# Loading q, k and v in float32 from another queue, casting on GpSimd, and two first layers ahead of the second

## The chip, the cores and the metric

The kernel runs on one core of one Trainium2 chip. What counts is the time of one execution in microseconds (us) on the device; several runs give a median. The profile of one execution gives a span, from its first to its last instruction. Engines: PE is TensorE (matmuls; PEld its weight loads), DVE is VectorE, ACT is ScalarE, POOL is GpSimd, SP is SyncE. PE, DVE, ACT, POOL and SP each run their own instructions in the order of their own queue and wait for one another by semaphores. Tiles lie in SBUF; PE writes into PSUM, which has eight banks per partition.

## What is computed

Causal attention with 8 heads of 64 over 768 positions, in 4 batches, followed by a feed-forward block whose activation is a squared ReLU. A query sees the 96 last positions (itself included) and the first 8 positions of the sequence; each head subtracts a slope times the distance from its scores (for the first positions, outside the window, the distance counts as 96).

```python
def _attn_ref(q, k, v, n_global, n_local):          # 4 x 8 x 768 x 64, 8, 96
    scores = scale * np.matmul(q, k.transpose(0, 1, 3, 2))
    rel = pos[:, None] - pos[None, :]
    is_global = pos[None, :] < int(n_global)
    is_local = (rel >= 0) & (rel < int(n_local))
    keep = is_global | is_local
    dist = np.where(is_global & ~is_local, float(n_local), np.abs(rel).astype(np.float32))
    scores = np.where(keep, scores - slopes[:, None, None] * dist[None], -1e9)
    a = softmax(scores)
    return np.matmul(a, v)

x = attn_out.transpose(0, 2, 1, 3).reshape(3072, 512)
h = np.maximum(x @ w_in, 0.0)                       # 512 x 2048
out = h * h @ w_out                                 # 2048 x 512
```

All inputs and the output are float32 in memory; inside, the matmuls take float16 and add up in float32.

## The kernel before

The work is cut into eight half batches (`hb` 0 to 7; `b, half = divmod(hb, 2)`), each with 384 query rows in three tiles of 128, and into four pairs of heads (`a` 0 to 3).

For each half batch `load` brings q, k and v: nine DMAs of one row tile each, issued on GpSimd's queue, which turn float32 into float16 on the way. q and k land in `sq` and `sk` (two buffers each), v lands in the batch's `v` tile, which has a column of ones beside each head. For the very first half batch each DMA takes four heads, so there are eighteen.

The attention of a half batch is a list of jobs. `fix_v` makes `vb`, a second form of the v tiles whose first 32 rows are those of the first positions. `prep(a)` transposes q and k of a pair on PE (`trp`), copies them out with ACT (`qk`) and builds `kb`, the corresponding second form of k, on DVE. `score` (two per pair) multiplies k with q into `sp`, ACT takes the exponential (`ex`), DVE multiplies by the mask (`phat`). `attend` multiplies `phat` with v into `av`, DVE divides by the sum (`rec`, `tm`). `to_x` transposes `tm` on PE and ACT copies it into `xt`. The list is skewed, so that `prep` of a pair stands before `score` of the one before it, and so on.

The feed-forward block of a half batch is another list: sixteen jobs `first` (layer 1: four matmuls each into `hps`; after each second one ACT makes `hr` by ReLU and DVE squares it into `h2`) and twelve jobs `second` (layer 2: four matmuls each into `yps`; DVE copies `y`, SP's queue stores it). `merge` spreads the attention of the next half batch over the feed-forward jobs of the present one. The PSUM pool for `sp`, `hps` and `yps` (`ps_big`) has three tiles, that for `trp`, `av` and `trx` two.

The masks (`fill_masks`) are made once, at the start: eight exponentials on ACT, and on DVE a few products over all eight heads. The weights, `w_in` and `w_out`, come in four parts each on GpSimd's queue, cast on the way.

Only PE's order is that of the program text (`manual_schedule(engines={PE})`); the other engines' instructions, DMA issues included, are put in order by the framework's scheduler from its own estimates.

Of the kernel before, what the change touches and what calls it, by code (L numbers as in the profile page):

```python
# [14 lines left out]
P = 128  # L15
# [17 lines left out]
def kernel(  # L33
# [22 lines left out]
    NHB = 2 * B  # L56
    GR = 32
# [16 lines left out]

    dist = const.tile([P, 2 * P], FP32, name="dist")
    distc = const.tile([P, 2 * P], FP32, name="distc")
# [3 lines left out]
    ge0 = const.tile([P, 2 * P], FP16, name="ge0")  # L80
    isg = const.tile([P, 1], FP32, name="isg")
    far = const.tile([P, 2 * P], FP16, name="far")
    decay = const.tile([P, H, 2 * P], FP16, name="decay")
    gw = const.tile([P, H, 2 * P], FP16, name="gw")
    cg = const.tile([P, H], FP16, name="cg")
# [3 lines left out]
    w_out_sb = const.tile([P, NFT, d_model], FP16, name="w_out_sb")  # L89

    def fill_index():
        nc.gpsimd.iota(dist, pattern=[[1, 2 * P]], base=0, channel_multiplier=-1,
                       allow_small_or_imprecise_dtypes=True)
        nc.gpsimd.iota(pidx, pattern=[[0, 1]], base=0, channel_multiplier=1,
                       allow_small_or_imprecise_dtypes=True)
        nc.vector.tensor_scalar(out=ident, in0=dist[:, 0:P], scalar1=0.0, scalar2=None,
                                op0=ALU.is_equal)

    def fill_masks():
        nc.vector.tensor_scalar(out=distc, in0=dist, scalar1=0.0, scalar2=None, op0=ALU.max)  # L100
        for h in range(H):
            nc.scalar.activation(out=decay[:, h, :], in_=distc, func=AF.Exp, scale=-slopes[h])
            nc.vector.memset(cg[:, h:h + 1], math.exp(-slopes[h] * NL))
        nc.vector.tensor_scalar(out=ge0, in0=dist, scalar1=0.0, scalar2=None, op0=ALU.is_ge)
        nc.vector.scalar_tensor_tensor(out=local, in0=dist, scalar=float(NL), in1=ge0,
                                       op0=ALU.is_lt, op1=ALU.mult)
        nc.vector.tensor_scalar(out=isg, in0=pidx, scalar1=float(NG), scalar2=None,
                                op0=ALU.is_lt)
        nc.vector.tensor_scalar(out=far, in0=local, scalar1=0.5, scalar2=isg,
                                op0=ALU.is_lt, op1=ALU.mult)  # L110
        nc.vector.tensor_tensor(out=gw, in0=far[:, None, :].to_broadcast([P, H, 2 * P]),
                                in1=cg[:, :, None].to_broadcast([P, H, 2 * P]), op=ALU.mult)
        own, bef = slice(0, P), slice(P, 2 * P)
        nc.vector.tensor_tensor(out=mask[:, :, P:3 * P], in0=decay,
                                in1=local[:, None, :].to_broadcast([P, H, 2 * P]), op=ALU.mult)
        nc.vector.tensor_tensor(out=mask[:, :, 0:P], in0=mask[:, :, P:2 * P],
                                in1=gw[:, :, own], op=ALU.add)
        nc.vector.tensor_tensor(out=mask[:, :, 2 * P:3 * P], in0=mask[:, :, 2 * P:3 * P],
                                in1=gw[:, :, bef], op=ALU.add)
        nc.vector.tensor_copy(out=mask[:, :, 3 * P:5 * P], in_=mask[:, :, P:3 * P])  # L120


# [4 lines left out]
    for b in range(B):  # L127
        bt = Batch()
        bt.sq = [None, None]
        bt.sk = [None, None]  # L130
        batches.append(bt)

    def load(b, half, h0, h1):
        bt = batches[b]
        if half == 0 and h0 == 0:
            bt.qk = qk_p.tile([P, 2, NPAIR, S], FP16, name="qk", tag="qk")
            bt.kb = qk_p.tile([P, NPAIR, NT - 1, P], FP16, name="kb", tag="kb")
            bt.v = qk_p.tile([P, NT, H, D + 1], FP16, name="v", tag="v")
            bt.vb = qk_p.tile([P, NT - 1, H, D + 1], FP16, name="vb", tag="vb")
            nc.vector.memset(bt.v[:, :, :, D:D + 1], 1.0)  # L140
        if h0 == 0:
            bt.sq[half] = stage_p.tile([P, HT, H, D], FP16, name="sq", tag="sq")
            bt.sk[half] = stage_p.tile([P, HT, H, D], FP16, name="sk", tag="sk")
# [17 lines left out]
    def prep(b, half, a):  # L161
        bt = batches[b]
        trp = ps_att.tile([P, 2, HT, P], FP16, name="trp", tag="att")
        for i, st in enumerate((bt.sq[half], bt.sk[half])):
            for t in range(HT):
                nc.tensor.transpose(out=trp[:, i, t, :], in_=st[:, t, 2 * a:2 * a + 2, :],  # L166
                                    identity=ident)
        nc.scalar.copy(out=bt.qk[:, :, a, half * HALF:(half + 1) * HALF],  # L168
                       in_=trp.rearrange("p i t c -> p i (t c)"))
        kt = bt.qk[:, 1, a, :].rearrange("p (t c) -> p t c", c=P)  # L170
        t0, t1 = (0, HT) if half == 0 else (HT, NT - 1)
        nc.vector.tensor_copy(out=bt.kb[:, a, t0:t1, GR:P], in_=kt[:, t0:t1, GR:P])  # L172
        nc.vector.tensor_copy(out=bt.kb[:, a, t0:t1, 0:GR],  # L173
                              in_=kt[:, 0:1, 0:GR].to_broadcast([P, t1 - t0, GR]))
# [67 lines left out]
    def attention(hb):  # L242
        b, half = divmod(hb, 2)
        A = list(range(NPAIR))
# [12 lines left out]


    def ffn(hb):
        t0 = hb * HALF  # L260
        st = {}
        jobs = []

        def first(i, m2):
            if i == 0 and m2 == 0:
                st["h2"] = h_p.tile([P, NFT, HALF], FP16, name="h2", tag="h2")
# [7 lines left out]
            if m2 == 1:  # L274
                hr = h_p.tile([P, 2, HALF], FP16, name="hr", tag="hr")
                nc.scalar.activation(out=hr, in_=st["ps"][:, :, 0:HALF], func=AF.Relu)  # L276
                nc.vector.tensor_tensor(out=st["h2"][:, 2 * i:2 * i + 2, :], in0=hr, in1=hr,
                                        op=ALU.mult)

        def second(j, m0):  # L280
            if j != 1 and m0 == 0:
                st["y"] = ps_big.tile([P, 2, 512], FP32, name="yps", tag="big")
            for m in range(m0, m0 + 4):
                nc.tensor.matmul(st["y"][:, j % 2, :], lhsT=st["h2"][:, m, j * P:(j + 1) * P],  # L284
                                 rhs=w_out_sb[:, m, :], start=m == 0, stop=m == NFT - 1)
            if m0 + 4 == NFT and j != 0:
                n = 2 if j == 1 else 1
                y = y_p.tile([P, 2, d_model], FP32, name="y", tag="y")
                nc.vector.tensor_copy(out=y[:, 0:n, :], in_=st["y"][:, 0:n, :])  # L289
# [4 lines left out]
        for i in range(NFT // 2):  # L294
            for m2 in range(2):
                jobs.append(lambda i=i, m2=m2: first(i, m2))
        for j in range(HT):
            for m0 in range(0, NFT, 4):
                jobs.append(lambda j=j, m0=m0: second(j, m0))
        return jobs  # L300
# [13 lines left out]
    fill_index()  # L314
    for h0 in range(0, H, 4):
        load(0, 0, h0, h0 + 4)
    fill_masks()
    for c in range(4):
        load_w_in(c)
    load(0, 1, 0, H)  # L320
    for c in range(4):
        load_w_out(c)
    load(1, 0, 0, H)
    with tc.manual_schedule(engines={PE}):
        for job in attention(0):
            job()
        for hb in range(NHB):
            if 1 <= hb and hb + 2 < NHB:
                load((hb + 2) // 2, hb % 2, 0, H)
            main = ffn(hb)  # L330
            side = attention(hb + 1) if hb + 1 < NHB else []
            for job in merge(main, side, 1, len(main) - 4):
                job()
# [35 lines left out]
```

## Time and profile before

| | |
|---|---|
| three runs | 260.56, 260.62 (median), 261.44 us |
| span of the profiled execution | 258.2 us |
| granted TensorE clock, mean | 0.986 of full speed |
| DMA on GpSimd's queue (q0) | 79,248 packets, 13.64 MB written |
| DMA on SP's queue (q1) | 3,328 packets, 6.29 MB written |
| read from HBM | 27.26 MB |

The profile gives no time of the execution other than its span; the median of the runs lies 2.4 us above it. A line of the groups reads: line of the program, engine, operation, output and inputs, shape and count; then busy time in us and the mean of one in ns; then the idle time ahead of them and what ended it. A window's line gives, after its length, each engine's busy time, the granted clock, the DMA share and GB/s as written. The slices cut the span into 40 parts of 6.5 us, with the busy share in tenths.

### The profile page before, as it was taken

Reading aid. Unit: us, or ns where it says so; the run is one execution under the profiler, and the core shown is the slowest. Engines: PE = TensorE matmul, PEld = TensorE weight load, DVE = VectorE, ACT = ScalarE, POOL = GpSimd, SP = SyncE. Lnnn points to the kernel's source line nnn. Section 1 sums busy time; section 2 is a strip of 40 time slices with the busy share of each in tenths; the row PEclk is TensorE's granted clock in tenths of the full one; section 3 lists DMA queues with packets and bytes.
Section 4 is the critical chain, followed back from the end, with each engine's and each line's share of the span. In section 5 each row is a group of like instructions: output and inputs, shape, how many; then the busy total and the mean of one; then the engine's idle time right before and its main releaser. Section 6 shows DMA issues by size and latency. Waiting matters only on the chain.

```text
span 258.2 us, 4590 instructions
## 1 busy us (share of the span) xinstructions
PE 227.6 (88%) x1888; PEld 125.0 (48%) x1888; DVE 139.6 (54%) x331; ACT 135.0 (52%) x201; POOL 75.9 (29%) x95
## 2 busy tenths in 40 slices
PE   1428769928999999999699999999999999999994
PEld 0216345514555555645455555655654565555541
DVE  8558237454778336746676436843675346543411
ACT  5436359601297329941587329831984179623600
POOL 8996573696207000528008000700000000000000
PEclk9999999985999999999999999999999999999999
DMA  6999999999909930499909630792100210003003
GB/s 44 87 116 205 169 179 208 156 153 109 209 1 63 62 121 3 29 96 76 169 3 84 41 122 3 50 76 81 43 0 0 85 41 3 0 5 119 0 3 122
DMA packets 82597, 20.22 MB, mean 78 GB/s; under 512 B 75408, under 2 KB 79504, under 8 KB 82576
## 3 DMA queue, kind: packets, MB, share of 16 engines
q0 software_dynamic: 79248, 13.64, 71.0%
q1 hardware_dynamic: 3328, 6.29, 6.6%
q8 instruction: 15, 0.25, 0.4%
q14 instruction: 6, 0.05, 0.1%
HBM read 27.26 MB, written 6.29 MB: 130 GB/s over the span
## 4 chain that ended last, share of the span: by engine, by line
PE 54%; DMA 17%; ACT 11%; POOL 11%; DVE 3%; issue 2%; DVEq 0%; POOLq 0%
PE yps L284 27%; PE hps L272 19%; DMA v<-in_v_dram 8%; POOL v L149 5%; DMA w_out_sb<-in_moe_w_out_dram 5%; DMA w_in_sb<-in_moe_w_in_dram 5%; ACT hr L276 4%; ACT ex L205 4%; PE av L220 3%; ACT qk L168 3%; PE sp L201 3%; POOL sq L149 2%; POOL sk L149 2%; PE trx L239 1%; POOL w_out_sb L310 1%
## 5 line engine op out<-in xcount | busy, mean ns | idle before, releaser
L272 PE MATMUL hps<-xt,w_in_sb 128*128 128x384 f16 x512 | 98.5, 329 | 2.6 <-DVE y L289 1.9
L276 ACT ACTIVATE hr<-hps 128x768 f16<-128x768 f32 x64 | 52.8, 825 | 43.9 <-PE hps L272 43.0
L272 PEld LDWEIGHTS <-w_in_sb 128*128 128x128 f16 x512 | 45.9, 98 | 31.4 <-issue 3.2
L205 ACT ACTIVATE ex<-sp 128x768 f16<-128x768 f32 x64 | 47.8, 779 | 8.9 <-PE sp L201 8.8
L149 POOL DMA_DIRECT2D sq<-in_q_dram x27 | 23.4, 882 | 71.0 <-PE trp L166 70.5
L206 DVE TENSOR_TENSOR phat<-ex,mask 128x768 f16<-128x768 f16 x64 | 33.0, 523 | 20.5 <-ACT ex L205 17.1
L240 ACT COPY xt<-trx 128x384 f16<-128x384 f16 x32 | 15.3, 478 | 41.1 <-PE trx L239 41.1
L168 ACT COPY qk<-trp 128x768 f16<-128x768 f16 x32 | 25.2, 808 | 15.3 <-PE trp L166 15.3
L289 DVE COPY y<-yps 128x1024 f32<-128x1024 f32 (+1 forms) x16 | 15.3, 958 | 26.3 <-PE yps L284 26.2
L149 POOL DMA_DIRECT2D v<-in_v_dram x27 | 23.3, 883 | 16.3 <-DVE rec L225 8.2
L149 POOL DMA_DIRECT2D sk<-in_k_dram x27 | 23.1, 878 | 4.1 <-DMA w_out_sb<-in_moe_w_out_dram 2.0
L220 PEld LDWEIGHTS <-phat 128*128 128x128 f16 x352 | 15.9, 102 | 16.4 <-DVE tm L227 6.2
L220 PE MATMUL av<-v,phat 128*128 128x65 f16 x192 | 16.4, 201 | 6.8 <-DVE tm L227 5.7
L166 PE MATMUL trp<-ident,sq 128*128 128x128 f16 x96 | 12.4, 229 | 7.4 <-DMA sq<-in_q_dram 7.4
L220 PE MATMUL av<-vb,phat 128*128 128x65 f16 x160 | 15.7, 200 | 3.3 <-DVE vb L157 3.3
L227 DVE TENSOR_TENSOR tm<-av,rec 128x384 f16<-128x384 f32 x32 | 17.8, 556 | 0.9
L201 PE MATMUL sp<-qk 64*128 64x128 f16 x192 | 17.7, 231 | 0.3 <-ACT qk L168 0.3
L201 PE MATMUL sp<-qk,kb 64*128 64x128 f16 x160 | 16.4, 227 | 1.7 <-DVE kb L173 1.7
L166 PE MATMUL trp<-ident,sk 128*128 128x128 f16 x96 | 12.4, 229 | 4.3 <-DMA sk<-in_k_dram 4.2
L172 DVE COPY kb<-qk 128x288 f16<-128x288 f16 (+1 forms) x32 | 10.2, 320 | 9.3 <-ACT qk L168 6.9
L201 PEld LDWEIGHTS <-qk 64*128 64x128 f16 x192 | 8.0, 97 | 14.8 <-issue 12.6
L166 PEld LDWEIGHTS <-sq 128*128 128x128 f16 x96 | 8.3, 101 | 12.3 <-DMA sq<-in_q_dram 8.8
(56 smaller groups left out, 246.6 us busy)
## 6 DMA issues: line engine op xcount, KB each, us to landing
out_dram<-y SPq DMA_DIRECT2D x8, 512.0 KB, 2.8
sq<-in_q_dram POOLq DMA_DIRECT2D x21, 128.0 KB, 5.7
sk<-in_k_dram POOLq DMA_DIRECT2D x21, 128.0 KB, 5.3
v<-in_v_dram POOLq DMA_DIRECT2D x21, 128.0 KB, 6.4
w_in_sb<-in_moe_w_in_dram POOLq DMA_DIRECT2D x4, 512.0 KB, 8.6
w_out_sb<-in_moe_w_out_dram POOLq DMA_DIRECT2D x4, 512.0 KB, 10.5
out_dram<-y SPq DMA_DIRECT2D x8, 256.0 KB, 2.0
sq<-in_q_dram POOLq DMA_DIRECT2D x6, 64.0 KB, 3.0
```

The lines of the kernel that those rows point to most:

```text
L149: nc.gpsimd.dma_start(out=dst[:, t, h0:h1, :], in_=src[b, h0:h1, r0:r0 + P, :].rearrange("h p d -> p h d"))
L166: nc.tensor.transpose(out=trp[:, i, t, :], in_=st[:, t, 2 * a:2 * a + 2, :], identity=ident)
L168: nc.scalar.copy(out=bt.qk[:, :, a, half * HALF:(half + 1) * HALF], in_=trp.rearrange("p i t c -> p i (t c)"))
L201: nc.tensor.matmul(sp[:, e, i * P:(i + 1) * P], lhsT=lhsT, rhs=bt.qk[rows, 0, a, r * P:(r + 1) * P], start=True, stop=True)
L205: nc.scalar.activation(out=ex[:, :, 0:n], in_=sp[:, :, 0:n], func=AF.Exp, scale=scale)
L206: nc.vector.tensor_tensor(out=phat[:, :, c0:c0 + n], in0=ex[:, :, 0:n], in1=mask[:, 2 * a:2 * a + 2, m0:m0 + n], op=ALU.mult)
L220: nc.tensor.matmul(av[:, e, j, :], lhsT=phat[:, e, i * P:(i + 1) * P], rhs=bt.vb[:, r - 1, h, :] if before else bt.v[:, r, h, :], start=n ...
L227: nc.vector.tensor_tensor(out=tm.rearrange("p t e d -> p e t d"), in0=av[:, :, :, 0:D], in1=rec[:, :, :, None].to_broadcast([P, 2, HT, D]) ...
L240: nc.scalar.copy(out=xts[hb][:, a, :], in_=trp.rearrange("p t c -> p (t c)"))
L272: nc.tensor.matmul(st["ps"][:, m2, 0:HALF], lhsT=w_in_sb[:, kk, m * P:(m + 1) * P], rhs=xt[:, kk, :], start=kk == 0, stop=kk == NCT - 1)
L276: nc.scalar.activation(out=hr, in_=st["ps"][:, :, 0:HALF], func=AF.Relu)
L284: nc.tensor.matmul(st["y"][:, j % 2, :], lhsT=st["h2"][:, m, j * P:(j + 1) * P], rhs=w_out_sb[:, m, :], start=m == 0, stop=m == NFT - 1)
```

## The change

q, k and v are now loaded without a cast: float32 goes into new `raw` tiles (six buffers for q and k, which take four heads each; six for v), on SP's queue, and for one half batch on ACT's. A piece of q or k is three successive rows of the sequence in one partition, 768 bytes in one run; v keeps its row tiles. GpSimd then casts into `sq`, `sk` (three buffers) and `v`; for the first half batch DVE casts q, two heads at a time. Since a transposed tile now holds every third row, ACT's copy into `qk` writes with a stride of three. The masks are made one pair at a time, between the casts and jobs of the first attention. `fix_v` moves behind `prep(1)`'s place in the list. Layer 1 of half batches 0 and 1 comes first, then layer 2 of half batch 0, with its parts of the inner sum in the outer loop, and of 1. `w_in` and `w_out` stay on GpSimd's queue with their cast: two parts of `w_in` ahead of the casts of the second half batch, the rest behind them. The order of every engine is the program's.

```diff
-    stage_p = ctx.enter_context(tc.tile_pool(name="stage", bufs=2))
+    raw_p = ctx.enter_context(tc.tile_pool(name="raw", bufs=6))
+    stage_p = ctx.enter_context(tc.tile_pool(name="stage", bufs=3))
...
+    def fill_mask(a):
+        hs = slice(2 * a, 2 * a + 2)
+        for h in (2 * a, 2 * a + 1):
+            nc.scalar.activation(out=decay[:, h, :], in_=distc, func=AF.Exp, scale=-slopes[h])
+        nc.vector.tensor_tensor(out=mask[:, hs, P:3 * P], in0=decay[:, hs, :],
+                                in1=local[:, None, :].to_broadcast([P, 2, 2 * P]), op=ALU.mult)
+        for h in (2 * a, 2 * a + 1):
+            nc.vector.scalar_tensor_tensor(
+                out=mask[:, h, 0:4 * P].rearrange("p (x c) -> p x c", c=2 * P)[:, :, 0:P],
+                in0=far.rearrange("p (x c) -> p x c", c=P), scalar=math.exp(-slopes[h] * NL),
+                in1=mask[:, h, P:3 * P].rearrange("p (x c) -> p x c", c=P),
+                op0=ALU.mult, op1=ALU.add)
+        nc.vector.tensor_copy(out=mask[:, hs, 3 * P:5 * P], in_=mask[:, hs, P:3 * P])
...
-        for src, dst in ((q, bt.sq[half]), (k, bt.sk[half]),
-                         (v, bt.v[:, half * HT:(half + 1) * HT, :, 0:D])):
-            for t in range(HT):
-                r0 = half * HALF + t * P
-                nc.gpsimd.dma_start(
-                    out=dst[:, t, h0:h1, :],
-                    in_=src[b, h0:h1, r0:r0 + P, :].rearrange("h p d -> p h d"))
+        for name, src in (("q", q), ("k", k)):
+            if o == 0:
+                bt.raw[half, name, g] = raw_p.tile([P, HH, HT, D], FP32, name="r" + name,
+                                                   tag="rqk")
+            (eng or nc.sync).dma_start(
+                out=bt.raw[half, name, g][:, o:o + n].rearrange("p h t d -> p h (t d)"),
+                in_=src[b, h0:h0 + n, rows, :].rearrange("h (p t) d -> p h (t d)", t=HT))
...
+    def load(b, half):
+        load_qk(b, half, 0, HH)
+        for t in range(HT):
+            load_v(b, half, t)
+        load_qk(b, half, HH, HH)
...
+    def cast(b, half):
+        if half == 0:
+            open_batch(b)
+        cast_qk(b, half, 0, HH, (nc.gpsimd, nc.gpsimd))
+        for t in range(HT):
+            cast_v(b, half, t)
+        cast_qk(b, half, HH, HH, (nc.gpsimd, nc.gpsimd))
...
-        nc.scalar.copy(out=bt.qk[:, :, a, half * HALF:(half + 1) * HALF],
-                       in_=trp.rearrange("p i t c -> p i (t c)"))
+        nc.scalar.copy(
+            out=bt.qk[:, :, a, half * HALF:(half + 1) * HALF].rearrange(
+                "d i (p t) -> d i t p", t=HT), in_=trp)
...
-        jobs = [lambda: fix_v(b, half)]
+        jobs = []
...
+            if a == 1:
+                jobs.append(lambda: fix_v(b, half))
...
-    with tc.manual_schedule(engines={PE}):
-        for job in attention(0):
+    with tc.manual_schedule():
+        fill_index()
+        for h0 in range(0, HH, 2):
+            load_qk(0, 0, h0, 2)
+        for t in range(HT):
+            load_v(0, 0, t)
+        for h0 in range(HH, H, 2):
+            load_qk(0, 0, h0, 2)
+        load(0, 1)
+        open_batch(0)
+        fill_mask(0)
+        att = attention(0)
+        for a in range(NPAIR):
+            cast_qk(0, 0, 2 * a, 2, (nc.vector, nc.gpsimd))
+            if a == 1:
+                for t in range(HT):
+                    cast_v(0, 0, t)
+            if a > 0:
+                fill_mask(a)
+            n = {0: 1, 1: 4, 2: 4, 3: len(att)}[a]
+            run(att[:n])
+            att = att[n:]
+        load_w_in(0)
+        load_w_in(1)
+        cast(0, 1)
+        load_w_in(2)
+        load_w_in(3)
+        for c in range(4):
+            load_w_out(c)
+        run(merge(layer_1(0), attention(1), 4, 15))
+        late = ([lambda: load_qk(1, 0, 0, HH, nc.scalar)]
+                + [lambda t=t: load_v(1, 0, t, nc.scalar) for t in range(HT)]
+                + [lambda: load_qk(1, 0, HH, HH, nc.scalar)])
+        run(merge(layer_1(1), late, 0, 10))
+        cast(1, 0)
+        load(1, 1)
+        run(merge(layer_2(0, True) + layer_2(1, False), attention(2), 2, 20))
+        for hb in range(2, NHB):
+            if hb + 1 < NHB:
+                cast((hb + 1) // 2, (hb + 1) % 2)
+            if hb + 2 < NHB:
+                load((hb + 2) // 2, hb % 2)
+            main = layer_1(hb) + layer_2(hb, False)
+            side = attention(hb + 1) if hb + 1 < NHB else []
+            run(merge(main, side, 1, len(main) - 4))
```

More of the change, by code (lines that the diff above doesn't have):

```diff
@@ L89 @@
     w_out_sb = const.tile([P, NFT, d_model], FP16, name="w_out_sb")
+    distc = h_p.tile([P, 2 * P], FP32, name="distc", tag="xt")
+    decay = h_p.tile([P, H, 2 * P], FP16, name="decay", tag="h2")
     def fill_index():
@@ L128, with load_qk @@
         bt = Batch()
[L129 to L130 removed]
+        bt.raw = {}
+        bt.sq = {}
         batches.append(bt)
[L133 removed]
+    def load_qk(b, half, h0, n, eng=None):
         bt = batches[b]
[L135 to L143, printed above, removed]
[L144 to L151 removed]
@@ new lines, in cast_v, with open_batch @@
+    def cast_v(b, half, t):
+        bt = batches[b]
+        nc.gpsimd.tensor_copy(out=bt.v[:, half * HT + t, :, 0:D], in_=bt.raw[half, "v", t])
+    def open_batch(b):
+        bt = batches[b]
+        bt.qk = qk_p.tile([P, 2, NPAIR, S], FP16, name="qk", tag="qk")
+        bt.kb = qk_p.tile([P, NPAIR, NT - 1, P], FP16, name="kb", tag="kb")
+        bt.v = qk_p.tile([P, NT, H, D + 1], FP16, name="v", tag="v")
+        bt.vb = qk_p.tile([P, NT - 1, H, D + 1], FP16, name="vb", tag="vb")
+        nc.gpsimd.memset(bt.v[:, :, :, D:D + 1], 1.0)
@@ L292, in second @@
                                   in_=y[:, 0:n, :])
[L294 to L300, printed above, removed]
+        order = ([(j, m0) for m0 in range(0, NFT, 4) for j in range(HT)] if by_part
+                 else [(j, m0) for j in range(HT) for m0 in range(0, NFT, 4)])
+        return [lambda j=j, m0=m0: second(j, m0) for j, m0 in order]
     def load_w_in(c):
@@ L312, in load_w_out, with run @@
             in_=moe_w_out[c * n * P:(c + 1) * n * P, :].rearrange("(m p) d -> p m d", p=P))
[L314 to L323, printed above, removed]
-    with tc.manual_schedule(engines={PE}):
-        for job in attention(0):
-            job()
[L327 to L330, printed above, removed]
+    def run(jobs):
+        for job in jobs:
+            job()
```

72 lines of the change are left out of this document (36 added, 36 removed).

## The prediction

> **What bounds the kernel now.** I read the page first: its busy shares and its slices.
>
> ```profile
> span 258.2 us, 4590 instructions
> PE 227.6 (88%) x1888; PEld 125.0 (48%) x1888; DVE 139.6 (54%) x331; ACT 135.0 (52%) x201; POOL 75.9 (29%) x95
> ...
> PE   1428769928999999999699999999999999999994
> DMA  6999999999909930499909630792100210003003
> ```
>
> PE is full from the eleventh slice on, except one; before that it is hungry while the DMA engines are full. So two regimes: a start fed by POOL's loads, then a PE that cannot be sped up. Next the windows of single half batches (layer 1, layer 2 and the next attention), which say how full the second regime is, and the pieces of the chain for the last one, which has no attention beside it.
>
> ```profile
> 121.90:151.69 29.79, 27.41 (x232) 14.90 (x229) 17.44 (x45) 16.27 (x24) 5.83 (x7) 1.00 0.80 87
> 151.69:179.21 27.52, 27.39 (x245) 15.27 (x244) 14.84 (x30) 16.61 (x24) 5.25 (x6) 1.00 0.53 59
> 179.21:206.22 27.01, 26.93 (x231) 14.81 (x229) 14.59 (x38) 15.90 (x24) 0.00 (x0) 1.00 0.08 31
> ...
> 94.59 2.62 PE hps L272 x16
> 233.74 10.40 PE hps L272 x64
> 244.14 10.37 PE yps L284 x48
> ```
>
> A half batch takes 27.0 to 27.5 us with PE busy throughout: 10.4 for layer 1, 10.4 for layer 2, so about 6.5 for an attention. Only 121.90 to 151.69 has a loss, 29.79 - 27.52 = 2.3 us. Then PE's timeline, for where the first half batches begin and where PE stops.
>
> ```profile
> 27.02 3.88 PE L272 MATMUL hps<-xt,w_in_sb 128*128 128x384 f16 x16
> 59.26 0.24 PE L220 MATMUL av<-v,phat 128*128 128x65 f16 x1 [5.71 <-DVE tm L227]
> 94.43 1.79 PE L272 MATMUL hps<-xt,w_in_sb 128*128 128x384 f16 x10
> ...
> DVE vb L159 <- DMA v<-in_v_dram: 8.6, 2, 5.5
> ```
>
> Layer 1 first runs at 27.02, the third half batch's at 94.43. Between them lie 67.4 us for two half batches whose work is 2 x 27.3 = 54.6: 12.8 lost. The last line is from the waits of the first 76 us (total, times, longest): DVE for v. DVE copies v of a later batch (`vb`, in an order not written by hand) before what the present one needs; PE's 5.71 us before 59.26 end with a `tm` that stood behind that. What can be gained is 27.0 (less the shortest start), 12.8 and 2.3 us.
>
> **The loads.** SP's queue carries only the output today, so the new loads' cost has no row of its own. The nearest:
>
> ```profile
> 10.00:12.00 2.00, 0.79 (x7) 0.34 (x7) 1.01 (x7) 1.05 (x2) 2.00 (x3) 1.00 1.35 86
> 22.00:24.00 2.00, 1.72 (x25) 1.17 (x23) 1.63 (x5) 2.00 (x5) 0.84 (x2) 1.00 1.24 205
> 50.00:52.00 2.00, 2.00 (x26) 1.19 (x26) 0.00 (x0) 0.81 (x1) 2.00 (x3) 1.00 2.43 155
> ...
> L291 SPq DMA_DIRECT2D out_dram<-y x16: 332/363/425, 65.0 to 255.3; - x16
> out_dram<-y SPq DMA_DIRECT2D x8, 512.0 KB, 2.8
> out_dram<-y SPq DMA_DIRECT2D x8, 256.0 KB, 2.0
> ```
>
> The last column of a window is GB/s written in float16, so twice that is read. At the start POOL, full (2.00 of 2.00), lets 86 through; later 155 with 256-byte source rows (q, k, v), 205 with weights among them (2 KB rows). Read side: 310 and 410 GB/s. The first half batch is 2.36 MB in float32: 5.8 to 7.6 us at these rates. SP issues a load in 0.36 us, 2 us to landing. q and k become 768-byte rows (three sequence rows in a piece, sorted back by the strided ACT copy), v keeps 256. I take 310 GB/s for v and between for q and k: pair 0 is there at about 3, v at 7, pair 3 at 9, where POOL today is still issuing at 12. The dear end: 256 rows take 0.8 us longer than 128, 6.2 ns a row; at that price 5,120 rows of a half batch (2,048 of q and k, 3,072 of v) take 32 us.
>
> The Trainium skill, "DMA: Bandwidth & Descriptors", section "Why small descriptors are slow (HBM only)", gives each packet three beats of overhead, 11 beats for 256 bytes. By that estimate 2 KB against 256 bytes is 64/67 against 8/11, a ratio of 1.31; the trace's 205/155 is 1.32, so it agrees, and q and k would run close to the weights' rate. The sum would not move, since below DVE, not the load, sets the start.
>
> **The start, on DVE in written order.** Durations (behind the bar: busy us, mean ns of one), and two pieces of the timeline:
>
> ```profile
> L206 DVE TENSOR_TENSOR phat<-ex,mask 128x512 f16<-128x512 f16 x16 | 6.7, 421 | 1.5 <-ACT ex L205 1.5
> L227 DVE TENSOR_TENSOR tm<-av,rec 128x384 f16<-128x384 f32 x32 | 17.8, 556 | 0.9
> L168 ACT COPY qk<-trp 128x768 f16<-128x768 f16 x32 | 25.2, 808 | 15.3 <-PE trp L166 15.3
> L172 DVE COPY kb<-qk 128x288 f16<-128x288 f16 x16 | 5.7, 354 | 2.9 <-ACT qk L168 2.0
> L173 DVE COPY kb<-qk 128x96 f16<-128x96 f16 x16 | 3.8, 246 | 0.0
> L157 DVE COPY vb<-v 64x1560 f16<-64x1560 f16 x4 | 2.6, 641 | 0.1
> L159 DVE COPY vb<-v 32x520 f16<-32x520 f16 x20 | 7.2, 409 | 9.6 <-DMA v<-in_v_dram 9.6
> L105 DVE SCALAR_TENSOR_TENSOR local<-dist,ge_87 128x256 f16<-128x256 f32 x1 | 0.4, 424 | 0.0
> L92 POOL IOTA dist<- 128x256 f32 x1 | 0.3, 336 | 0.4 <-POOLq L350 0.4
> L225 DVE RECIPROCAL rec<-av 128x6 f32<-128x6 f32 x32 | 6.3, 196 | 11.2 <-PE av L220 11.2
> L240 ACT COPY xt<-trx 128x384 f16<-128x384 f16 x32 | 15.3, 478 | 41.1 <-PE trx L239 41.1
> L276 ACT ACTIVATE hr<-hps 128x768 f16<-128x768 f32 x64 | 52.8, 825 | 43.9 <-PE hps L272 43.0
> ...
> 2.33 0.29 DVE L109 TENSOR_SCALAR far<-local,isg 128x256 f16<-128x256 f16 x1
> 8.06 0.53 PE L166 MATMUL trp<-ident,sq 128*128 128x128 f16 x3
> ```
>
> The masks, made at once today while POOL loads, are now four parts between the casts. One part: a product of 512 (0.42), two scalar_tensor_tensors of 256 (0.42 each), a copy (0.35): 1.6 us. A q cast (384 elements, nearest `tm`): 0.55. `kb` 0.60. The `vb` copies 2 x 0.64 + 3 x 0.41 = 2.5, now behind prep(1) and ahead of every `phat`. Two `phat` products about 1.0; reciprocal and `tm` 0.75. The index work ends at 2.6 as today, mask 0 at 4.3, cast 0 at 4.9; six transposes 0.9 at the pace of the three at 8.06, the ACT copy 0.8; `kb` ends at 7.2. Cast 1 and mask 1 until 9.3, `kb` 10.1; `vb` 12.6; `phat` of pair 0, 13.6. Pair 2's cast, mask, `kb` (behind transposes and an ACT copy), `phat` of pair 1, `tm` of pair 0: 18.6. The same round for pair 3: 23.4. `phat` of pair 3, two last `tm`: 26.2. Transposes and the `xt` copy: 27.2. Layer 1 starts where it does today, 27.02: the faster load buys nothing there, since masks 2 and 3 and `vb`, 5.7 us, stand in DVE's queue behind waits. Inputs of pairs 2 and 3 may come at 13 and 18 before that grows.
> POOL's casts have no row; the iota, 0.34 for 256, is 1.3 ns an element with its fixed part. So at most 0.5 for a k piece, 0.7 for a v tile, 1.0 for four heads, 6 us per half batch if a cast runs as an iota does; I take that, and twice that as the far bound. In the full stages they lie beside DVE, a stage ahead of their reader.
>
> **The two first half batches.** Layer 1(0) with attention(1): 10.4 + 6.5, plus the cold PE (16 matmuls took 3.88 at 27.02, 2.62 later): 1.3. Behind the last `ex` stand `phat`, `av`, `tm`, transposes, `xt`: 2.4 us with under one us of layer 1 left, so 1.5 of stall. End 46.7. `w_in` parts 2 and 3 wait on POOL behind the casts of the second half batch; its data land near 21, so they are issued at 23 and land before 30; job 8 needs them near 35: hidden, with 5 us of cover. `w_out` lands behind them near 40, needed at 57. Layer 1(1) alone: 10.4, ending at 57.1; ACT has 8 `hr` of 0.83 and 7 issues of 0.36 there, 9.2. Its DMAs reuse buffers freed long before. Layer 2(0) and 2(1) with attention(2): 20.8 + 6.5, and since layer 2(0) by parts holds two of three big PSUM tiles, each score waits for the `ex` before it, which takes about as long as an `hr`, 0.83, and has some 0.5 of other matmuls beside it: 0.3 us some five times, 1.5. End 85.9. Today that point is 94.43: **-8.5**. The `vb` stall at 121.90 cannot come back, as fix_v stands in its own half batch: **-2.3**. For order and casts in the full stages I add **+1.0** (bounds 0, and six stages x 0.7 = 4, a held-up DVE instruction each). SP's output stores stand behind loads that wait for raw buffers; those are freed by casts a stage earlier: 0. Sum -9.8: span 248.4. The median, 260.62, stands 2.4 above the span: forecast **250.8 us**.
>
> **Rivals.**
> *Blocking.* DVE and POOL hold each other up. `vb` L157 has a longest of 0.87 at 18.40, when POOL was issuing:
>
> ```profile
> 18.40 0.87 DVE L157 COPY vb<-v 64x1560 f16<-64x1560 f16 x1
> ```
>
> against 0.64 in the mean. POOL's casts within the start (4 k, 3 v: 4 us) would then fall on DVE's chain, and some 0.7 in each of six full half batches (DVE has 16 of 27 busy): 4 + 4 - 1.0 taken already, 258. The Trainium skill, "SBUF — State Buffer", section "Who interferes with whom", says that the one issued second waits for the whole of the first. By it this rival would be the rule; the trace shows the slowing but not a full wait.
> *Ends slower: rows are dear on SP's queue.* At 4 ns a row a half batch takes 20.5 us: pair 3 lands at 23 and layer 1 starts near 32; the second half batch lands at 44, POOL casts it, and only then issues `w_in` 2 and 3, which land at 49 to 52 with PE stopped at job 8: two half batches end near 97, 262. That is its point; at 6.2 ns every stage is load-bound, 8 x 32 and more, above 280. For it: no load has yet run there. Against: 256-byte rows already pass at 310 GB/s, 0.8 ns a row.
> *The early start.* DVE waits less than written and the masks are quicker: layer 1 at 23, the rest as in the forecast: 247.
> *Nothing changes:* the stalls in order take back the 9.8: 260.
>
> **How the numbers follow.** 0.5% (1.3 us) is about what a measurement of this kernel tells from no change. Forecast 0.40, early start 0.14, blocking 0.20 (all faster: 0.74), nothing 0.06, dear rows 0.20. The range, 245.5 to 264, leaves out the far part of dear rows and a start below 22.
>
> **What would show it.** PE's first `hps` near 27; `w_in` landed before job 8, no DMA wait of PE between 30 and 57; `hps` of the third half batch near 86; stages of 27.0 to 27.8; no wait of DVE for v behind that. Wrong: a DMA wait of POOL's casts past 25, or `phat` far above 0.56 us.

## The result: 0.7% slower, where 4% faster was forecast

| | us (median, lowest to highest) | runs |
|---|---|---|
| before | 261.21 (259.76 to 261.87) | 11 |
| changed | 262.98 (261.74 to 265.75) | 11 |
| forecast | 250.8 (245.5 to 264) | |

The ratio of changed to before is 1.0073, with a 95% interval of 1.0047 to 1.0099: a small loss, but clear of the scatter. The profiled execution of the changed kernel is its slowest, 265.75 us; its span is 263.1, and all its stages are read against that.

The page of the changed kernel: busy time by engine, PE's slices, the chain that ended last by line, and one group.

```profile
PE 225.8 (86%) x1888; PEld 126.5 (48%) x1888; DVE 152.4 (58%) x334; ACT 152.3 (58%) x201; POOL 64.4 (24%) x74
...
PE   1237797799988997999889988999799988999994
...
PE yps L331 29%; PE hps L309 18%; ACT qk L205 8%; DVE phat L244 5%; ACT hr L313 3%; PE av L258 3%; PE sp L239 2%; ACT ex L243 2%; DVE h L314 2%; PE trx L277 2%; DVE vb L195 2%; DVE vb L193 2%; DVE mask L115 2%; PE trp L203 2%; DVE kb L210 2%
...
L205 ACT COPY qk<-trp 128x768 f16<-128x768 f16 x32 | 46.5, 1453 | 16.6 <-PE trp L203 15.6
```

Where the slices of before had a row of nines with a single 6 in it, there is now a 7 or an 8 in nearly every half batch. The last line is what is new. The ACT copy of the transposed q and k, 808 ns before, takes 1453: 32 x 0.645 = 20.6 us more on ACT, and it stands on the chain with 8%.

PE's timeline shows the marks that the prediction named, and the small stops within one of the full stages (a bracket is the idle time ahead of a row and what ended it).

```profile
29.42 6.01 PE L309 MATMUL hps<-xt,w_in_sb 128*128 128x384 f16 x20
93.28 1.95 PE L309 MATMUL hps<-xt,w_in_sb 128*128 128x384 f16 x11
129.06 0.23 PE L239 MATMUL sp<-qk 64*128 64x128 f16 x2 [0.82 <-ACT hr L313]
132.99 0.81 PE L309 MATMUL hps<-xt,w_in_sb 128*128 128x384 f16 x4 [0.65 <-ACT ex L243]
137.64 0.23 PE L239 MATMUL sp<-qk 64*128 64x128 f16 x2 [0.22 <-ACT hr L313]
238.23 3.09 PE L309 MATMUL hps<-xt,w_in_sb 128*128 128x384 f16 x18
```

Layer 1 first runs at 29.42 (forecast 27.2), the third half batch's at 93.28 (85.9), the last one's at 238.23. The windows say how full PE is between these marks and in one stage, and how full ACT is in that stage's first half (busy time and count of PE, PEld, DVE, ACT, POOL, then clock, DMA share, GB/s).

```profile
29.42:93.28 63.86, 57.78 (x475) 32.05 (x474) 35.08 (x76) 37.98 (x49) 15.10 (x19) 1.00 0.66 141
93.28:238.23 144.95, 136.37 (x1190) 75.92 (x1188) 86.85 (x192) 92.40 (x120) 33.97 (x29) 1.00 0.35 93
122.47:151.16 28.69, 27.00 (x229) 14.90 (x228) 18.05 (x39) 18.03 (x24) 9.38 (x8) 1.00 0.39 111
124.00:139.50 15.50, 13.81 (x134) 8.20 (x133) 12.43 (x28) 14.65 (x18) 9.38 (x8) 1.00 0.63 170
```

The stage has 27.00 us of PE work, about as before (26.93 to 27.41 in the prediction's windows), and lasts 28.69. The three stops above, 0.82 + 0.65 + 0.22 = 1.69, are the whole difference. They lie in its first half, where layer 1's `hr` and the attention's `qk` and `ex` meet on ACT: 14.65 of 15.50 us busy. Over the whole stage ACT is busy for 18 of 29, which is why its share on the page (58%) does not look like a bound. ACT's own timeline there:

```profile
124.96 1.45 ACT L205 COPY qk<-trp 128x768 f16<-128x768 f16 x1 [0.17 <-PE trp L203]
126.22 0.83 ACT L313 ACTIVATE hr<-hps 128x768 f16<-128x768 f32 x1
126.95 1.43 ACT L205 COPY qk<-trp 128x768 f16<-128x768 f16 x1
128.17 0.84 ACT L313 ACTIVATE hr<-hps 128x768 f16<-128x768 f32 x1
128.90 1.29 ACT L243 ACTIVATE ex<-sp 128x768 f16<-128x768 f32 x2
```

From 125 on there is no gap between the rows; the `hr` that ends at 129.0 frees the PSUM tile for which PE's `sp` waited 0.82. Over the whole span the two kinds of wait add up to 9.0 us (total, times, longest); the list of the kernel before has neither:

```profile
PE sp L239 <- ACT hr L313: 4.6, 10, 0.8
PE hps L309 <- ACT ex L243: 4.4, 8, 0.7
```

### The profile page after: what moved, and what is told of

Read it like the earlier page. It is cut to its first block, busy times and chain, and to the rows that moved or that the text cites. A ratio compares the mean times of both kernels' runs of the same rounds, so it can differ in the third digit from the quotient of the medians.

```text
span 263.1 us, 4695 instructions
## 1 busy us (share of the span) xinstructions
PE 225.8 (86%) x1888; PEld 126.5 (48%) x1888; DVE 152.4 (58%) x334; ACT 152.3 (58%) x201; POOL 64.4 (24%) x74
## 4 chain that ended last, share of the span: by engine, by line
PE 56%; DVE 22%; ACT 14%; issue 6%; POOL 0%; ACTq 0%; POOLq 0%
PE yps L331 29%; PE hps L309 18%; ACT qk L205 8%; DVE phat L244 5%; ACT hr L313 3%; PE av L258 3%; PE sp L239 2%; ACT ex L243 2%; DVE h L314 2%; PE trx L277 2%; DVE vb L195 2%; DVE vb L193 2%; DVE mask L115 2%; PE trp L203 2%; DVE kb L210 2%
## 5 line engine op out<-in xcount | busy, mean ns | idle before, releaser
L331 PE MATMUL yps<-w_out_sb,h 128*128 128x512 f16 x384 | 93.5, 379 | 1.1 <-DVE y L336 1.1
L309 PEld LDWEIGHTS <-w_in_sb 128*128 128x128 f16 x512 | 47.2, 99 | 34.6 <-issue 6.9
L205 ACT COPY qk<-trp 128x768 f16<-128x768 f16 x32 | 46.5, 1453 | 16.6 <-PE trp L203 15.6
L314 DVE TENSOR_TENSOR h<-hr 128x768 f16<-128x768 f16 x64 | 37.7, 590 | 31.8 <-ACT hr L313 31.0
L331 PEld LDWEIGHTS <-h 128*128 128x128 f16 x384 | 33.8, 98 | 33.5 <-issue 1.1
L244 DVE TENSOR_TENSOR phat<-ex,mask 128x768 f16<-128x768 f16 x64 | 36.4, 585 | 14.2 <-ACT ex L243 12.6
L165 POOL CAST sq<-rq 128x768 f16<-128x768 f32 x14 | 14.0, 998 | 108.3 <-DMA rq<-in_q_dram 69.1
L336 DVE COPY y<-yps 128x1024 f32<-128x1024 f32 (+1 forms) x16 | 15.3, 957 | 27.9 <-PE yps L331 27.8
L171 POOL CAST v<-rv 128x512 f16<-128x512 f32 x24 | 26.7, 1129 | 11.3 <-DMA rv<-in_v_dram 11.2
L203 PE MATMUL trp<-ident,sq 128*128 128x128 f16 x96 | 11.3, 230 | 16.1 <-DVE sq L165 16.1
L165 POOL CAST sk<-rk 128x768 f16<-128x768 f32 (+1 forms) x18 | 16.8, 934 | 10.3 <-DMA rk<-in_k_dram 9.0
```

The costliest lines, as they stand in the source:

```text
L165: eng.tensor_copy(out=bt.sq[half, name, g][:, :, o:o + n, :].rearrange("p t h d -> p h t d"), in_=bt.raw[half, name, g][:, o:o + n])
L171: nc.gpsimd.tensor_copy(out=bt.v[:, half * HT + t, :, 0:D], in_=bt.raw[half, "v", t])
L203: nc.tensor.transpose(out=trp[:, i, t, :], in_=bt.sq[half, name, g][:, t, o:o + 2, :], identity=ident)
L244: nc.vector.tensor_tensor(out=phat[:, :, c0:c0 + n], in0=ex[:, :, 0:n], in1=mask[:, 2 * a:2 * a + 2, m0:m0 + n], op=ALU.mult)
L309: nc.tensor.matmul(st["ps"][:, m2, 0:HALF], lhsT=w_in_sb[:, kk, m * P:(m + 1) * P], rhs=xt[:, kk, :], start=kk == 0, stop=kk == NCT - 1)
L314: nc.vector.tensor_tensor(out=h2s[hb][:, 2 * i:2 * i + 2, :], in0=hr, in1=hr, op=ALU.mult)
```

## Experiments

Theory A: the write of `qk` with a step of three elements costs ACT 0.65 us a copy, and ACT then sets the pace wherever layer 1 and an attention overlap. Theory B: GpSimd's casts hold up DVE's instructions, as the first rival had it. The first four kernels tell them apart, and whether it is the writing or the reading of a step that costs.

**The write in one run, rows left as they come** (`no_stride`; this leaves out the sorting):

```diff
-                "d i (p t) -> d i t p", t=HT), in_=trp)
+                "d i (t p) -> d i t p", t=HT), in_=trp)
```

> The changed kernel with one edit: the ACT copy into qk writes its rows in one run, so the three row tiles stay unsorted (this leaves out the sorting of the rows; all durations are otherwise those of the change). Theory A (the strided copy, 1.45 us against 0.81, is what the forecast left out): the copy is back at 0.8 us, the full half batches fall from 29.1 to 27.3-27.6 us (5 x 1.7 = 8.5), the first two from 63.9 to about 59, and the time is 248 to 251 us. Theory B (DVE and POOL holding each other up is the larger loss): only the direct saving on the start's chain, 4 x 0.65 = 2.6, and a little in the half batches: 257 to 260 us.

Measured: 249.02 us (246.31 to 249.39), ratio 0.950 (0.9435 to 0.9565); the copy takes 807 ns.

**The step moved from the write to the read** (`strided_read`); everything is computed:

```diff
-                "d i (p t) -> d i t p", t=HT), in_=trp)
+                "d i (p t) -> d i p t", t=HT),
+            in_=trp.rearrange("d i t p -> d i p t"))
```

> The changed kernel, with the sorting moved to the read side of the same copy: ACT reads PSUM with a stride and writes qk in one run. Theory A1 (the writes in steps of 6 bytes cost): as no_stride, copy 0.8 us, 248 to 251 us. Theory A2 (any stride on either side costs): copy 1.45 us, 262 to 264 us. Theory B: 257 to 260.

Measured: 247.46 us (246.5 to 250.02), ratio 0.948 (0.9409 to 0.9547); run again beside a later kernel, 248.12 and 0.9525 (0.9493 to 0.9557). The profile is of the execution of 250.02 us, span 247.9: its group on the page, rows of PE's timeline, and the windows between the marks:

```profile
L205 ACT COPY qk<-trp 128x768 f16<-128x768 f16 x32 | 25.8, 807 | 17.1 <-PE trp L203 16.7
```

```profile
27.47 6.02 PE L310 MATMUL hps<-xt,w_in_sb 128*128 128x384 f16 x20
46.95 0.20 PE L259 MATMUL av<-v,phat 128*128 128x65 f16 x1 [1.37 <-DVE tm L266]
69.99 0.23 PE L240 MATMUL sp<-qk 64*128 64x128 f16 x2 [0.36 <-ACT ex L244]
86.83 2.11 PE L310 MATMUL hps<-xt,w_in_sb 128*128 128x384 f16 x12
```

```profile
27.47:86.83 59.36, 57.17 (x475) 31.36 (x474) 33.81 (x76) 33.55 (x49) 16.70 (x22) 1.00 0.73 156
86.83:223.02 136.19, 135.67 (x1189) 75.00 (x1188) 88.21 (x192) 82.12 (x120) 34.32 (x29) 1.00 0.37 99
```

The read with the step costs nothing (807 ns). Of the two waits for PSUM tiles above, 0.3 us is left, and PE is busy for 135.67 of 136.19 us in the five full stages. Set against the changed kernel: 29.42 - 27.47 = 1.95 us in the start, 63.86 - 59.36 = 4.50 in the two first half batches, 144.95 - 136.19 = 8.76 in the five stages, nothing behind; in sum 15.2, which is the difference of the spans, 263.1 - 247.9. This version beats both kernels.

**The stepped write alone, in the kernel before** (`before_strided`; the same two lines as the change has them):

> The kernel before with one edit: its copy into qk writes in steps of three elements (this puts the rows out of their order). Theory A: ACT gets 0.65 x 4 = 2.6 us more per half batch, the full half batches go from 27.0-27.5 to about 29, six of them, and the start is later by 2: 270 to 274 us. Theory B (the copy is beside other work and costs little): 261 to 263 us.

Measured: 274.78 us (273.55 to 277.2), ratio 1.051 (1.042 to 1.060). That is just above the range of theory A, as the full half batches take 29.8 to 31.4 us where about 29 was expected. Its group, and PE's two waits for PSUM tiles, which the kernel before does not have:

```profile
L168 ACT COPY qk<-trp 128x768 f16<-128x768 f16 x32 | 46.2, 1444 | 16.6 <-PE trp L166 11.4 <-DVE kb L174 3.2 <-DVE kb L173 2.0
```

```profile
PE sp L202 <- ACT hr L277: 10.2, 14, 1.6
PE hps L273 <- ACT ex L206: 4.1, 6, 0.7
```

With no load, cast or order changed, 32 x 0.636 = 20.4 us more of this copy on ACT cost 13.7 us. Theory A holds from both sides: put in, it costs 5%; taken out, it gives 6%. Theory B is not needed for the result.

**q and k in row tiles of 256 bytes, so that nothing is to be sorted** (`row_tiles`):

```diff
-            (eng or nc.sync).dma_start(
-                out=bt.raw[half, name, g][:, o:o + n].rearrange("p h t d -> p h (t d)"),
-                in_=src[b, h0:h0 + n, rows, :].rearrange("h (p t) d -> p h (t d)", t=HT))
+            for t in range(HT):
+                r0 = half * HALF + t * P
+                (eng or nc.sync).dma_start(
+                    out=bt.raw[half, name, g][:, o:o + n, t, :],
+                    in_=src[b, h0:h0 + n, r0:r0 + P, :].rearrange("h p d -> p h d"))
...
-                "d i (p t) -> d i t p", t=HT), in_=trp)
+                "d i (t p) -> d i t p", t=HT), in_=trp)
```

> The changed kernel with q and k loaded as row tiles of 256-byte rows, three DMAs where there was one, and the copy into qk in one run; all is computed. Theory A: the copy is at 0.8 us and the load is hidden but for the start, where SP issues 24 pieces of q and k instead of 8 (16 x 0.47 = 7.5 us later for pair 3): 249 to 255 us. Theory B: 257 to 262 us.

Measured: 259.06 us (258.06 to 261.46), ratio 0.993 (0.9891 to 0.9967). From GpSimd's timeline, and from the waits (total, times, longest):

```profile
36.10 0.83 POOL L167 CAST sk<-rk 128x768 f16<-128x768 f32 x1 [1.45 <-PE sp L241]
36.88 1.48 POOL L349 DMA_DIRECT2D w_in_sb<-in_moe_w_in_dram  x2
```

```profile
PE hps L311 <- DMA w_in_sb<-in_moe_w_in_dram: 4.7, 1, 4.7
```

q and k now have three times as many issues and three times as many rows. The second half batch comes late, its casts end at 36.9 (the last of them most likely waits for k, which SP issues only from 31.45 on), and `w_in` parts 2 and 3, queued behind them, leave PE standing for 4.7 us: the mechanism of the rival of dear rows. On ACT's queue the issues for a later half batch hold up two `hr` by 3.8 and 3.9 us, and PE stops for 1.6 and 2.0 us behind them. How much is due to the number of issues and how much to the shorter rows was not separated. The time lies in the range of theory B (257 to 262), but not by its mechanism: the full stages take 26.9 to 27.4 us here, since the copy writes in one run.

**Every cast of GpSimd made twice** (`casts_twice`; from here on the edits are made on the strided read):

```diff
-            eng.tensor_copy(
-                out=bt.sq[half, name, g][:, :, o:o + n, :].rearrange("p t h d -> p h t d"),
-                in_=bt.raw[half, name, g][:, o:o + n])
+            for _ in range(1 if eng is nc.vector else 2):
+                eng.tensor_copy(
+                    out=bt.sq[half, name, g][:, :, o:o + n, :].rearrange("p t h d -> p h t d"),
+                    in_=bt.raw[half, name, g][:, o:o + n])
...
-        nc.gpsimd.tensor_copy(out=bt.v[:, half * HT + t, :, 0:D], in_=bt.raw[half, "v", t])
+        for _ in range(2):
+            nc.gpsimd.tensor_copy(out=bt.v[:, half * HT + t, :, 0:D], in_=bt.raw[half, "v", t])
```

> The kernel with the strided read of PSUM, with each of GpSimd's casts made twice, so that GpSimd is busy 5 to 6 us more per half batch; nothing is left out. If the strided write by ScalarE was the whole of what the forecast missed, and casts on GpSimd only slow VectorE where VectorE is itself late: the first hps moves from 27.5 to about 31 (the k casts and v casts of the start stand in its chain), the full stages stay at 27.0 to 27.6, and the time is 250 to 252. If VectorE and GpSimd hold each other up in full: each stage of a half batch grows by 2 to 3 us, phat's 512 form goes above 0.7 us, and the time is 262 or more.

Measured: 256.57 us (256.18 to 257.84), ratio 0.982 (0.9779 to 0.9867), between the two expectations. GpSimd's casts take 107 us in place of 57, and the first `hps` is at 31.80. Three groups of DVE, of the strided read first and then with the casts doubled:

```profile
L245 DVE TENSOR_TENSOR phat<-ex,mask 128x768 f16<-128x768 f16 x48 | 28.3, 599 | 10.7 <-ACT ex L244 9.7
L245 DVE TENSOR_TENSOR phat<-ex,mask 128x512 f16<-128x512 f16 x16 | 8.4, 523 | 1.6 <-ACT ex L244 1.6
L266 DVE TENSOR_TENSOR tm<-av,rec 128x384 f16<-128x384 f32 x32 | 17.8, 558 | 1.1
```

```profile
L247 DVE TENSOR_TENSOR phat<-ex,mask 128x768 f16<-128x768 f16 x48 | 31.7, 669 | 7.3 <-ACT ex L246 6.2
L247 DVE TENSOR_TENSOR phat<-ex,mask 128x512 f16<-128x512 f16 x16 | 13.1, 816 | 0.6 <-ACT ex L246 0.5
L268 DVE TENSOR_TENSOR tm<-av,rec 128x384 f16<-128x384 f32 x32 | 17.8, 558 | 1.1
```

`phat`, with both inputs in SBUF, grows from 599 to 669 ns and from 523 to 816; `tm`, which reads PSUM, stays at 558. The Trainium skill, "SBUF — State Buffer", section "Who interferes with whom", says that an instruction of VectorE with two inputs in SBUF contends with a GpSimd instruction that reads SBUF; the three rows agree with that. Rows with one input in SBUF moved both ways: the small `kb` copies (128x96) went from 264 to 367 ns, the ones of 128x192 from 362 to 257. Of the 254.6 - 247.9 = 6.7 us, 31.80 - 27.47 = 4.33 lie in the start, where the casts also stand in the chain themselves. A full stage hides nearly all of it: 27.2 to 27.5 us. So of the two signs of full blocking one came, `phat`'s 512 form above 0.7 us, and the other, stages longer by 2 to 3 us, did not. Blocking is real, but small in the time: what one set of casts costs was not measured by itself.

**The layers in the old order** (`layers_old_order`):

```diff
-        run(merge(layer_1(0), attention(1), 4, 15))
+        load(1, 0)
+        run(merge(layer_1(0) + layer_2(0, False), attention(1), 1, 24))
...
-        run(merge(layer_2(0, True) + layer_2(1, False), attention(2), 2, 20))
+        run(merge(layer_1(1) + layer_2(1, False), attention(2), 1, 24))
```

> The kernel with the strided read of PSUM, with the order of the layers undone: layer 1 and layer 2 of the first half batch with the attention of the second, then both layers of the second with the attention of the third, each merged in order as in the later stages. If the gain of the change lies in loads and casts in a written order: third half batch's layer 1 at 84 to 88 (strided read: 87.0), time 245 to 249. If it lies in having the two layers 1 first: layer 2 of the first half batch needs w_out at about 45, and the attention of the third needs its casts by 56, so PE stops, the third half batch starts at 91 or later, time 252 or more.

The edit also moves the load of the third half batch from ACT's queue back to SP's. Measured: 251.99 us (249.58 to 252.38), ratio 0.961 (0.9544 to 0.9673). The two waits of PE behind the start:

```profile
48.37 1.02 PE L332 MATMUL yps<-w_out_sb,h 128*128 128x512 f16 x4 [2.23 <-DMA w_out_sb<-in_moe_w_out_dram]
51.05 1.75 PE L332 MATMUL yps<-w_out_sb,h 128*128 128x512 f16 x4 [1.38 <-DMA w_out_sb<-in_moe_w_out_dram]
```

Layer 2 then comes before `w_out`: 3.6 us of waits, and the third half batch starts at 88.6, between the two expectations. The new order of the layers is worth some 3 us by the spans (250.6 against 247.9); the intervals of the ratios overlap a little, so this is likely rather than shown.

**The written order for PE alone** (`pe_order_only`):

```diff
-    with tc.manual_schedule():
+    with tc.manual_schedule(engines={PE}):
```

> The kernel with the strided read of PSUM, with the written order kept for TensorE alone, and the other engines ordered by the scheduler as in the kernel before. If the written order of VectorE, ScalarE and GpSimd brings nothing by itself: 246 to 249, no wait of VectorE for v. If it is what took away the v stalls: vb copies of a later half batch stand ahead of phat or tm again, VectorE waits 5 us or more for v, and the time is 252 to 262.

Measured: 269.15 us (267.36 to 270.65), ratio 1.029 (1.0226 to 1.036), worse than either expectation. PE's longest stop in its timeline, and the wait behind it:

```profile
52.35 0.29 PE L240 MATMUL sp<-qk,kb 64*128 64x128 f16 x2 [11.40 <-DVE kb L211]
```

```profile
DVE vb L195 <- POOL v L171: 13.8, 2, 13.0
```

The scheduler put a `vb` copy of a v that was not there ahead of `kb`, and PE stood for 11.4 us. It is of the kind that the prediction read in the kernel before (5.71 us there), twice as long. The full stages behind it take 26.9 to 27.4 us, as with the written order. With these loads the order written out by hand is worth 269.15 - 247.46 = 21.7 us, more than the whole gain of the strided read over the kernel before.

**Attempts on the start.** `late_copy` makes the mask's copy for the second half batch once, behind the first attention. `quiet_start` also issues all of `w_in` first and holds the next casts back until the masks are done:

```diff
-        nc.vector.tensor_copy(out=mask[:, hs, 3 * P:5 * P], in_=mask[:, hs, P:3 * P])
...
+        for c in range(4):
+            load_w_in(c)
+        nc.gpsimd.tensor_copy(out=mask[:, H - 1, 4 * P:4 * P + 8], in_=mask[:, H - 1, 2 * P:2 * P + 8])
+        nc.vector.tensor_copy(out=mask[:, :, 3 * P:5 * P], in_=mask[:, :, P:3 * P])
         cast(0, 1)
```

> The kernel with the strided read of PSUM, with the mask's second copy (columns 384 to 640, read first by the second half batch) made once for all heads behind the first attention in place of four times within it. If the start is bound by VectorE's chain as forecast: its four copies (0.29 to 0.87 us each, 2.3 in all) leave it, the first hps goes from 27.5 to 25.2 and the time from 247.5 to 245.2. If the start is bound by loads or ScalarE: first hps stays at 27.2 to 27.5, time 247 to 248.

> The kernel with the late mask copy, with all four w_in loads issued first, and with GpSimd's casts of the second half batch held behind the masks of pair 3 (by a copy of eight of its columns on GpSimd), so that they no longer lie at 14.6 to 17.8 beside VectorE's chain. If GpSimd's casts beside VectorE are what kept the late copy from paying: its rows there go back to what they take alone (mask product 1.03 to 0.42, two mask sums 1.39 to 0.76, kb 0.87 to 0.25 and 1.13 to 0.17: 2.8 us), the first hps goes from 26.7 to about 23.9 and the time to 243 to 245. If VectorE's chain is held by ScalarE or the loads there: first hps stays at 26 to 27, time 246 to 249.

> The kernel with the strided read of PSUM, unchanged, beside the one with the quiet start on one chip, so that their difference can be read: 246.5 to 248.5 us, first hps at 27.5.

Measured: `late_copy` 248.13 us, ratio 0.950 (0.9435 to 0.9558); `quiet_start` 248.76, 0.957 (0.9538 to 0.9597); the strided read again 248.12, 0.9525. The first `hps` is at 26.66 and 26.73, that of the strided read again at 26.56. Neither brings anything that can be measured. DVE in the quiet start shows why:

```profile
14.42 0.76 DVE L115 SCALAR_TENSOR_TENSOR mask<-far,mask 128x256 f16<-128x256 f16 x2
15.80 0.26 DVE L210 COPY kb<-qk 128x288 f16<-128x288 f16 x1 [0.62 <-ACT qk L204]
...
20.58 0.78 DVE L211 COPY kb<-qk 128x96 f16<-128x96 f16 x1
21.28 1.74 DVE L244 TENSOR_TENSOR phat<-ex,mask 128x768 f16<-128x768 f16 x2
```

Against the late copy the instructions at 14 to 16 do shrink (the two mask sums from 1.39 to 0.76, `kb` from 0.87 to 0.26), but DVE then waits 0.62 for `qk`, and the casts fall on pair 3 instead (0.78 for a `kb` of 0.17, 1.74 for two `phat`). The start is a chain through PE, ACT and DVE, not DVE's sum alone.

**What a step costs, by itself** (`act_strides`): copies of 768 elements a partition behind the last half batch, three of each form in one execution.

> The kernel with the strided read of PSUM, and behind its last half batch copies of 768 elements a partition, three of each form, on ScalarE and then VectorE and GpSimd: written with a step of 1, 2, 3 and 4 float16 elements, as pairs of neighbours with a gap of two, as float32 with a step of 1 and 3, and read with a step of 3 and written in one run. Only the duration of each copy is of interest, not the time of the kernel, which grows by some 45 us; the copies change nothing of the output. If single float16 elements written apart go at half the rate whatever the step: ScalarE takes 1.45 us at steps 2, 3 and 4, and 0.81 for step 1, for pairs and for both float32 forms. If it is the step of 6 bytes, which falls across 4-byte words: 1.45 at step 3 alone, 0.81 at steps 2 and 4. If any gap between writes costs: pairs and float32 with a step of 3 take 1.45 too. A read with a step of 3 takes 0.81 from PSUM, as in the kernel; from SBUF no run has shown it. VectorE and GpSimd: step 3 takes up to twice step 1 if the cost is on the side of SBUF, and as step 1 if it is ScalarE's own.

The groups (busy us, mean ns of one); `src_psum` lies in PSUM, `src_sbuf` in SBUF, `read_three` reads with a step of three and writes in one run; output f16 or f32 as shown:

```profile
L424 ACT COPY act_f_step_one<-src_psum 128x768 f16<-128x768 f16 x3 | 2.4, 800 | 0.1
L427 ACT COPY act_f_step_two<-src_psum 128x768 f16<-128x768 f16 x3 | 3.0, 1011 | 0.1
L430 ACT COPY act_f_step_three<-src_psum 128x768 f16<-128x768 f16 x3 | 4.3, 1433 | 0.1
L433 ACT COPY act_f_step_four<-src_psum 128x768 f16<-128x768 f16 x3 | 5.6, 1868 | 0.1
L437 ACT COPY act_f_pairs<-src_psum 128x768 f16<-128x768 f16 x3 | 2.5, 831 | 0.1
L443 ACT CAST act_f_step_three<-src_psum 128x768 f32<-128x768 f16 x3 | 3.5, 1169 | 0.1
L464 DVE COPY dve_f_step_three<-src_psum 128x768 f16<-128x768 f16 x3 | 4.3, 1425 | 0.1
L495 POOL COPY pool_sb_step_three<-src_sbuf 128x768 f16<-128x768 f16 x3 | 4.4, 1462 | 0.2
L455 ACT COPY act_sb_read_three<-src_sbuf 128x768 f16<-128x768 f16 x3 | 2.5, 833 | 0.1
L489 DVE COPY dve_sb_read_three<-src_sbuf 128x768 f16<-128x768 f16 x3 | 2.8, 948 | 0.1
```

None of the three accounts fits. The price grows with the step (0.80, 1.01, 1.43, 1.87 us for 1 to 4), so neither half rate nor 6 bytes explains it; pairs of neighbours with a gap cost 0.83, so a gap alone does not; float32 with a step of 12 bytes costs 1.17, less than float16 with 6. From PSUM, VectorE takes the same 1.43 for the stepped write, and GpSimd from SBUF 1.46, so it is not ScalarE's own. The free read is not common to all: VectorE takes 948 ns to read from SBUF with a step of three, against 356 in one run and 805 for the stepped write from SBUF; from PSUM the read takes 950, against 558 in one run.

## Why the prediction was wrong

The step that failed is one term: the ACT copy. The prediction let the pieces of q and k be "sorted back by the strided ACT copy" and put "the ACT copy 0.8" into the start, from the row of the copy before, 808 ns. That row is of another access pattern. The price of the new one stood in no row, and it was given no bounds; the +1.0 us for "order and casts", with bounds of 0 and 4, covered a held-up DVE and nothing on ACT. Measured, 1453 ns. Taken at 1.45 it adds 4 x 0.645 = 2.6 us of ACT to a stage, in the half in which eight `hr` and the `ex` of the attention take turns with three PSUM tiles; 1.76 of it came through (28.69 against 26.93 for the same stage of the strided read). None of the rivals had it. The slower one had the sign, by a mechanism that appears only in `row_tiles`; that its 262 lies beside the measured 262.98 is chance.

With that term put right (`strided_read`), the steps stand thus:

- **The start**: 27.2 forecast, 27.47 and 26.56 measured in two executions; 29.42 with the slow copy. The load itself, as said, bought nothing there. It was slower than put: pair 3's k was there at 12.9 us, not at 9, and an issue took 0.47 us for two heads of q or k and 1.1 for a v tile, not 0.36. That stayed inside the bound of 18.
- **The first two half batches**: third `hps` at 85.9 forecast, 86.83 measured. Within, two errors cancel. For layer 1(0) with attention(1) the prediction's terms add up to 19.7 us (its end at 46.7 counts from 27.0, not from 27.2). The 68 matmuls from 48.55 begin with the last four of this layer, so it ended at 49.2 and took 21.7. The stall in it was 1.37, near the 1.5 put down (the row at 46.95); but the first 20 matmuls took 6.02 us where 20 of those 68, which take 11.21 us in all, need 3.3: a slow beginning of 2.7, not 1.3. Against that, the stall of layer 2 by parts, put at 1.5, is one wait of 0.36 (the row at 69.99).
- **`w_in` behind the casts is hidden**: PE waits for no DMA from 30 to 57, in the changed kernel too. `row_tiles` shows what happens when the cover is gone.
- **The v stall of 2.3 us** in a full stage is gone, but it is gone in `pe_order_only` too, so the written order of the other engines is not needed for that; which part of the change did it stays open. What the written order takes away is the stall in the first two half batches.
- **Stages** of 27.0 to 27.8 forecast, 26.92 to 27.45 measured. The sum, span 248.4, against 247.9.
- **Casts**: put at up to 0.5, 0.7 and 1.0 us, they took 0.75, 1.13 and 0.99 in the changed kernel; two of the three groups:

```profile
L165 POOL CAST sk<-rk 128x384 f16<-128x384 f32 x4 | 3.0, 745 | 5.8 <-DMA rk<-in_k_dram 5.8
...
L171 POOL CAST v<-rv 128x512 f16<-128x512 f32 x24 | 26.7, 1129 | 11.3 <-DMA rv<-in_v_dram 11.2
```

The shortest took 0.50, 0.61 and 0.82, so the estimate fits the fastest casts; in the mean it was too low by up to 60%, and that cost nothing in the full stages, where they lie beside PE.

- **The signs**: one sign of being wrong, a DMA wait of GpSimd's casts past 25, did appear, and meant nothing. In the strided read a cast waits 22.48 us for q up to 54.38, because ACT issues that load only at 50.77, and PE waits for none of it.

## What to carry to other kernels

A row of the profile prices an instruction only together with its access pattern: where an edit gives an instruction another step, treat it as a new operation with bounds of its own, and ask which engine it loads in which stage. An engine at 58% of the span can be the bound for half of every stage; look at the window where its work is dense. And where a step cannot be avoided in a copy on ScalarE, try it on the side that is read: that one edit turned 0.7% slower into 5% faster. On VectorE price both sides first: from SBUF its read with a step of three (948 ns) was dearer than the write (805).

## What was not expected of the hardware

On ScalarE a write of single float16 elements apart from each other cost up to 2.3 times a write in one run (1868 against 800 ns at a step of four), a read with a step of three nothing (833 ns from SBUF, against 832 in one run; 807 from PSUM in the kernel). The Trainium skill, "SBUF — State Buffer", section "Specifications (TRN2)", states that a 16-byte line needs at least two hits for full bandwidth. By that, as an estimate from its figure, a step of two, three or four float16 elements would be free; ScalarE's read with a step of three agrees (833 against 832 ns), VectorE's read (948 against 356) and the writes do not, and the measurement decides. Why the price rises with the step, and why float32 pays less, stays open.
